# Opening of a gated state-space and MLP kernel rearranged: a B tile loaded transposed, the gate product two groups later, scan tables mirrored from half their length

## The chip, the cores and the metric

The kernel runs on one core of one Trainium2 chip. The metric is the device time of one execution in microseconds. The median of three runs of the kernel before is 551.43 us (551.0 to 551.49).

## The reference, cut to what matters

The input x has 2048 rows (time steps) of 1024 features. The result is a gate g times a state-space branch a, plus (1 - g) times an MLP branch b. The gate is a sigmoid of one weighted row sum of x.

```python
g = sigmoid((x * gate_w).sum(-1, keepdims=True))
dt = exp(log_dt); Lam_bar = exp(dt * Lam)              # complex, 1024 states
B_bar = ((Lam_bar - 1) / Lam)[:, None] * (B_re + 1j * B_im)
Bu = einsum("bld,pd->blp", x, B_bar)
h_t = Lam_bar * h_{t-1} + Bu_t                         # for all 2048 steps
a = 2 * einsum("blp,dp->bld", h, C_re + 1j * C_im).real + x * Dskip
b = gelu(layernorm(x) @ w1 + b1) @ w2 + b2
out = g * a + (1 - g) * b
```

## The kernel before

**Stages on the matrix engine (PE).** PE runs four stages: the u stage, which multiplies x by B (real and imaginary part) and gives the input u of the scan; the MLP's first and second product; and the y stage, which multiplies the scanned state by C. VectorE (DVE) runs the scan behind the later stages, with cosine and sine tables that it builds from 256 positions for each of the 1024 states.

**Groups.** Nearly every product is done as a 2 x 2 block product with seven sub-products instead of eight. The class `SG` holds them as p1 to p7; in the u stage each is four matmuls of 512 columns. They need sums of the operands: `b_sums` makes S1 to S4 from B, `x_sums` and `x_sum4` make T1 to T4 from x (tiles `xqo(pr, i)`; T4 takes the place of a raw part of x). p5 takes S1 and T1, p6 S2 and T2, p7 S3 and T3, p4 the raw A22 and T4, p3 S4. A group `bu_group(pt, pr)` covers tile pt of B (128 states, real and imaginary part) and half pr of x (1024 rows). The order is (1,0), (2,0), (3,0), (0,1), (1,1), ... and from the third group on it goes: p1 of this group, p7 of the one before, p5 and p6 of this one, p4 of the one before, p2 and p3 of this one. p7 and then p4 of one group add into the same PSUM bank, and the value between them is one half of u: ScalarE copies it out (`uc`, L1221) and VectorE adds the part of `s5` to it (L1223). Tile 0 with half 0 is done by plain products (`bu_plain`).

**Transposed operands.** PE needs x and B with the features on the partitions. At the opening the first 512 rows of x (`t_x`, four tiles) and tiles 0 to 3 of B (`t_b0`, `t_b`) are loaded as they lie, transposed on PE against an identity in eight steps a tile, and copied out of PSUM by VectorE or ScalarE. The other 1536 rows of x come through three transposing DMAs (`xT_dma`, L1232, chunks 1 to 3 of 512 rows), and tiles 4 to 7 of B through transposing DMAs later (`bT_dma`, L1316). Loads are issued on SP's queue, the small vectors (`cst_loads`) on ScalarE's, and stores on GpSimd's.

**The gate product.** `z_gate` (L1289) multiplies all of x, so all three transposed chunks, by the gate weight in 32 matmuls, four of them side by side in the array. It stands in the second group (n == 1 of the loop), ahead of `x_sum4(0)`, since that one overwrites raw x. `z_move` sends the row through HBM into a column layout; the layer norm waits for it.

**Order of the work.** Nothing is placed by hand on an engine. Each task has a duration and a priority, and a planner (`Graph.schedule`) works out one order for each engine; on PE the chain `pe_last` fixes the order of products, while `o_chain` does so for the opening. Every engine then runs its list in order. At the start PE runs nine idle products on zeros (`em_warm`).

Of the kernel before, what the change touches and what calls it, by code (L numbers as in the profile page):

```python
# [43 lines left out]
def c_dve(N):  # L44
    return 0.09 + N / 960.0
# [126 lines left out]
class Graph:  # L172
# [43 lines left out]
    def dma(self, prio, emit, nbytes, sem, reads=(), writes=(), name="", xpose=False, extra=(), ndma=1, bw=None, thr=False, q="sp"):  # L216
# [3 lines left out]
        if xpose:  # L220
            idur = max(idur, XPOSE_ISSUE_PER_MB * nbytes / 1e6)
        return self.add(q, idur, prio, emit, reads, writes, name, kind="dma", nbytes=nbytes,
                        sem=sem, xpose=xpose, extra=extra, ndma=ndma, bw=bw, thr=thr)

    def _schedule_once(self):
# [27 lines left out]
        while ev:  # L253
# [17 lines left out]
            for e in engs:  # L271
# [25 lines left out]
                if t.kind == "dma":  # L297
                    issue_end = st + t.dur
                    push(issue_end, 1, e)
                    ts = max(issue_end, chan_free[e])  # L300
                    busy_o = sum(1 for o in chan_free if o != e and chan_free[o] > ts)
                    bw_eff = t.bw * (1.0, 0.55, 0.4)[busy_o]
                    chan_free[e] = ts + t.nbytes / bw_eff
                    t.finish = chan_free[e] + DMA_LAT
# [76 lines left out]
    def _schedule_latest(self, ls):  # L381
# [57 lines left out]
        while ev:  # L439
# [8 lines left out]
            for e in engs:  # L448
# [13 lines left out]
                if t.kind == "dma":  # L462
                    issued = t.start + t.dur
                    push(issued, 1, e)
                    ts = max(issued, chan_free[e])
                    others = sum(1 for o in chan_free if o != e and chan_free[o] > ts)
                    chan_free[e] = ts + t.nbytes / (t.bw * (1.0, 0.55, 0.4)[others])
                    t.finish = chan_free[e] + DMA_LAT
# [97 lines left out]
def build(nc, A_x, A_Lambda_re, A_Lambda_im, A_B_re, A_B_im, A_C_re, A_C_im, A_log_dt, A_Dskip,  # L566
# [25 lines left out]
    with es:  # L592
# [81 lines left out]
        tfirst = [7, 3, 6, 0, 1, 2, 5]  # L674
# [57 lines left out]
        g.dma(P0, emit_cst_loads, NROW * 256, sem("d_cst"), writes=[b_stg], name="cst_loads", ndma=len(vecs), q="act")  # L732
# [36 lines left out]
        def load_x(k, prio):  # L769
            v = XNAT[k]  # L770
            g.dma(prio, lambda e: e.dma_start(out=v.ap, in_=x2[k * 128:(k + 1) * 128, :]), 128 * D * 2,  # L771
                  ssem("xnat", k), writes=[v], name="xnat%d" % k)
# [3 lines left out]
        def load_b(pt, prio):  # L776
# [9 lines left out]
            g.dma(prio, em, 2 * 128 * D * 2, ssem("bnat", s), writes=[v], name="bnat%d" % pt, ndma=2)  # L786
# [4 lines left out]
        def t_x(k, prio):  # L791
# [11 lines left out]
            o_chain(g.add("pe", 0.06 * DT, prio, em, reads=[v, b_ident], writes=[b_ps[bk], b_ps[bk2]], name="xT_T%d" % k, extra=list(o_last)))  # L803
# [12 lines left out]
        def t_b(pt, prio):  # L816
            s = pt % 4
            for ri in range(2):
                bk = tbank()

# [8 lines left out]
                if (pt, ri) == (1, 1):  # L829
# [23 lines left out]
        def load_b0(ri, prio):  # L853
# [3 lines left out]
            g.dma(prio, lambda e: e.dma_start(out=v.ap, in_=ap[0:128, :]), 128 * D * 2, ssem("bnatA", ri), writes=[v], name="bnat0.%d" % ri)  # L857
# [3 lines left out]
        for k in range(1, 4):  # L861
            load_x(k, (-0.9, k))
        load_b0(1, (-0.89, 0))
        for pt in range(1, 4):
            load_b(pt, (-0.85, pt))

        def t_b0(ri, prio):
# [8 lines left out]
            t = g.add("pe", 0.06 * DT, prio, em, reads=[v, b_ident], writes=[b_ps[bk]], name="bT0.%d" % ri, extra=list(o_last))  # L876
            if ri == 0:
                o_chain(t)
            o = AR.v(bqo(0, 2 * ri), [(1, D)])
            if ri == 0:  # L880
                first_a.append(g.add("act", c_act(D), prio, lambda e: e.activation(o.ap, V(PS16[bk], 0, [(1, D)]), AF.Copy),
                                     reads=[b_ps[bk]], writes=[o, b_ps[bk]], name="bTe0.0"))
            else:
                first_e.append(g.add("dve", 0.65, prio, lambda e: e.tensor_copy(o.ap, V(PS16[bk], 0, [(1, D)])),
                                     reads=[b_ps[bk]], writes=[o, b_ps[bk]], name="bTe0.1"))
# [3 lines left out]
        for k in range(1, 4):  # L889
            t_x(k, (-0.8, k + 1))  # L890
        t_b0(1, (0.6, 0))
        bk0 = tbank()
        g.add("pe", 0.06, (0.6, 1),
              lambda e: e.transpose(V(PS16[bk0], 0, [(1, NROW)]), V(STG, 0, [(1, 128)], npart=NROW), V(IDENT, 0, [(1, NROW)], npart=NROW)),
              reads=[b_stg, b_ident], writes=[b_ps[bk0]], name="cst_T", extra=list(o_last))
        stage_names = ["LRE", "LIM", "LDT", "DSK", "B2", "GW", "B1"]
        cst_cp = g.add("dve", 0.15, P0, lambda e: e.tensor_copy(V(CST, 0, [(1, NROW)]), V(PS16[bk0], 0, [(1, NROW)])),
              reads=[b_ps[bk0]], writes=[bc(n) for n in stage_names] + [b_ps[bk0]], name="cst_copy", extra=first_e[-1:])

# [4 lines left out]
        dv("dt_exp", lambda e: e.activation(C("DTC", 0, n8), C("LDT", 0, n8), AF.Exp), ["LDT"], ["DTC"], dur=0.3, eng="act", prio=P0)  # L904
        b_dtb = B("dtb")
        g.add("dve", 0.12, P0, lambda e: e.tensor_copy(V(DTB, 0, [(1, n8)]), C("DTC", 0, n8)), reads=[bc("DTC")], writes=[b_dtb], name="dt_b16")
        g.add("dve", 0.12, P0, lambda e: e.tensor_copy(C("DTC", 0, n8), V(DTB, 0, [(1, n8)])), reads=[b_dtb], writes=[bc("DTC")], name="dt_back")
        dv("a", lambda e: e.tensor_tensor(C("A", 0, n8), C("DTC", 0, n8), C("LRE", 0, n8), ALU.mult), ["DTC", "LRE"], ["A"], prio=P0)
        dv("th", lambda e: e.tensor_tensor(C("TH", 0, n8), C("DTC", 0, n8), C("LIM", 0, n8), ALU.mult), ["DTC", "LIM"], ["TH"], prio=P0)
        dv("r_exp", lambda e: e.activation(C("R", 0, n8), C("A", 0, n8), AF.Exp), ["A"], ["R"], dur=0.3, eng="act", prio=P0)  # L910
        b_ki = B("ki")
        b_ki2 = B("ki2")
        dv("phi", lambda e: e.tensor_scalar(C("PHI", 0, n8), C("TH", 0, n8), 1.0 / TWO_PI, None, ALU.mult), ["TH"], ["PHI"], prio=P0)
        g.add("dve", 0.12, P0, lambda e: e.tensor_copy(V(KI, 0, [(1, n8)]), C("PHI", 0, n8)), reads=[bc("PHI")], writes=[b_ki], name="ki")
        g.add("dve", 0.12, P0, lambda e: e.tensor_copy(C("KF2", 0, n8), V(KI, 0, [(1, n8)])), reads=[b_ki], writes=[bc("KF2")], name="kf")
        dv("ttr", lambda e: e.tensor_tensor(C("TTR", 0, n8), C("PHI", 0, n8), C("KF2", 0, n8), ALU.subtract), ["PHI", "KF2"], ["TTR"], prio=P0)
# [1030 lines left out]
```

## Time and profile before

| what | us |
|---|---|
| median of three runs | 551.43 |
| profiled execution | 554.73 |
| span of the profiled execution | 553.0 |
| PE busy in the span | 546.1 |
| DVE busy in the span | 510.2 |
| ScalarE (ACT) busy in the span | 287.1 |

The profiled execution took 1.73 us more than its span, and 3.30 us more than the median; differences are worked out inside the span and taken off the median. A busy PE is not a PE at its peak: ends of matmuls are modelled, and a stretch at a lower clock is busy too. The spans of PE's weight loads (PEld) show the real spacing of its instructions.

### The profile page before, as it was taken

What the parts mean: (1) busy time and instruction counts of PE and PEld (TensorE: products, weight loads), DVE (VectorE), ACT (ScalarE), POOL (GpSimd) and SP (SyncE); (2) the same over time, 40 slices, a digit from 0 to 9 for tenths busy, and PEclk for the clock granted to TensorE, in tenths of its full rate; (3) what the DMA queues carried; (4) which work ended last, traced back from release to release, by engine and by line L of the source; (5) the groups of instructions that cost most, each with busy time, mean ns of one, the idle gap of its engine ahead of it and who ended that gap; (6) DMA issues with size and microseconds to landing.
All of it is one profiled execution on the core that took longest, in us unless ns stands there. A gap on an engine that the chain in (4) does not pass through costs nothing.

```text
span 553.0 us, 7464 instructions
## 1 busy us (share of the span) xinstructions
PE 546.1 (99%) x2622; PEld 250.2 (45%) x2622; DVE 510.2 (92%) x880; ACT 287.1 (52%) x480; POOL 89.7 (16%) x146
## 2 busy tenths in 40 slices
PE   8899999999999999999999999999999999999997
PEld 5444444444444444444444444444444444444443
DVE  5879989999999999999999999999999999899863
ACT  3767887886773347773347762247672322111110
POOL 0127662540001010001110000220000111001000
PEclk9989999999999999999999999999999999999999
DMA  9996999789762455464666983797767999987531
GB/s 268 252 301 155 272 272 293 252 274 360 237 142 105 164 190 206 148 216 196 225 227 184 310 167 64 135 200 226 240 157 136 230 312 298 376 293 249 180 117 57
DMA packets 115054, 120.07 MB, mean 217 GB/s; under 512 B 70338, under 2 KB 92738, under 8 KB 113994
## 3 DMA queue, kind: packets, MB, share of 16 engines
q1 hardware_dynamic: 102400, 73.69, 47.9%
q0 software_dynamic: 12480, 45.90, 26.8%
q8 instruction: 20, 0.33, 0.2%
q14 instruction: 16, 0.13, 0.1%
q10 hardware_dynamic: 138, 0.02, 0.0%
HBM read 56.40 MB, written 47.46 MB: 188 GB/s over the span
## 4 chain that ended last, share of the span: by engine, by line
PE 94%; SPq 3%; DMA 2%; issue 0%; DVE 0%
PE ps L1034 71%; PE ps L1032 22%; SPq L1232 2%; DMA ar<-in_A_x_dram 2%; PE ps L1289 1%; PE ps L1100 0%; SPq L771 0%; SPq L784 0%; SPq L783 0%; SPq L857 0%; DVE ar L1732 0%
## 5 line engine op out<-in xcount | busy, mean ns | idle before, releaser
L1034 PE MATMUL ps<-ar 128*128 128x512 f16 (+1 forms) x1844 | 416.9, 379 | 0.0
L1034 PEld LDWEIGHTS ps<-ar 128*128 128x128 f16 (+1 forms) x1844 | 180.1, 98 | 218.1 <-issue 1.3
L1032 PE MATMUL ps<-ar 128*128 128x512 bf16 (+1 forms) x608 | 150.0, 379 | 0.0
L1119 DVE TENSOR_TENSOR ar<-ar 128x512 f16<-128x512 bf16 (+7 forms) x224 | 140.0, 662 | 3.9 <-PE ps L1289 2.0
L1032 PEld LDWEIGHTS ps<-ar 128*128 128x128 bf16 (+1 forms) x608 | 59.3, 98 | 71.5 <-ACT ar L833 0.4
L1426 DVE TENSOR_TENSOR_SCAN ar<-cst,init,ar 128x256 bf16<-128x256 f32 x128 | 88.1, 734 | 0.4
L1054 ACT ACTIVATE ar<-ps 128x512 f32<-128x512 f32 x102 | 59.8, 596 | 51.1 <-PE ps L1032 36.8
L1070 ACT ACTIVATE ps<-ps 128x512 f32<-128x512 f32 x67 | 39.0, 582 | 75.4 <-PE ps L1032 64.3
L1412 DVE TENSOR_TENSOR ar<-ar 128x2048 bf16<-128x2048 bf16 x64 | 77.0, 1217 | 0.2 <-ACT ar L1000 0.2
L1533 ACT ACTIVATE ar<-ps,cst 128x512 bf16<-128x512 f32 x56 | 38.4, 686 | 13.4 <-PE ps L1034 13.1
L1055 ACT ACTIVATE ar<-ps,cst 128x512 f32<-128x512 f32 x32 | 22.0, 688 | 44.6 <-PE ps L1034 22.1
L1622 ACT ACTIVATE ar<-ps,cst 128x512 f32<-128x512 f32 x32 | 22.0, 687 | 43.6 <-PE ps L1034 43.6
L1415 DVE TENSOR_TENSOR ar<-ar 128x1024 bf16<-128x1024 bf16 x64 | 42.0, 683 | 0.1
L1539 ACT ACTIVATE ar<-ar,cst 128x512 bf16<-128x512 f32 x56 | 40.0, 713 | 3.7 <-DVE ar L1537 3.5
L1537 DVE TENSOR_TENSOR ar<-ps,ar 128x512 f32<-128x512 f32 x56 | 38.2, 683 | 3.8 <-PE ps L1034 3.1
L1136 POOL DMA_DIRECT2D scr_u<-ar x32 | 24.9, 780 | 44.4 <-ACT ar L1164 20.4
L1745 DVE SCALAR_TENSOR_TENSOR ar<-ps,cst,ar 128x512 bf16<-128x512 f32 x31 | 22.6, 741 | 6.2 <-PE ps L1034 6.0
L1634 POOL DMA_DIRECT2D scr_ac<-ar x16 | 13.8, 892 | 87.5 <-ACT ar L1055 26.1
L1444 POOL DMA_DIRECT2D scr_h<-ar x16 | 9.4, 586 | 108.8 <-DVE ar L1415 88.7
L1625 DVE SCALAR_TENSOR_TENSOR ar<-ps,cst,ar 128x512 f32<-128x512 f32 x32 | 23.6, 741 | 3.5 <-PE ps L1034 2.9
L1632 POOL DMA_DIRECT2D scr_ac<-ar x16 | 8.5, 534 | 83.9 <-DVE ar L1625 54.8
L1716 DVE SCALAR_TENSOR_TENSOR ar<-ar,cst 128x1024 f32<-128x1024 bf16 x16 | 20.1, 1273 | 0.0
(120 smaller groups left out, 248.0 us busy)
## 6 DMA issues: line engine op xcount, KB each, us to landing
scr_ac<-ar POOLq DMA_DIRECT2D x32, 512.0 KB, 5.4
ar<-in_A_x_dram SPq DMA_DIRECT2D x32, 256.0 KB, 5.0
scr_u<-ar POOLq DMA_DIRECT2D x32, 256.0 KB, 5.1
ar<-scr_u SPq DMA_DIRECT2D x16, 512.0 KB, 4.5
scr_h<-ar POOLq DMA_DIRECT2D x16, 512.0 KB, 4.5
ar<-scr_ac SPq DMA_DIRECT2D x16, 512.0 KB, 7.5
ar<-scr_h SPq DMA_DIRECT2D x8, 1024.0 KB, 7.0
ar<-in_B_w_dram SPq DMA_DIRECT2D x14, 512.0 KB, 5.5
```

What stands on the lines that cost most here:

```text
L1032: ins = e.matmul(V(PS[bk], 0, [(1, n)]), st[i].ap, mv[i].ap, start=(i == 0), stop=(i == K - 1))
L1034: ins = e.matmul(V(PS[bk], 0, [(1, n)]), st[i].ap, mv[i].ap, start=False, stop=(i == K - 1), skip_group_check=True)
L1054: return e.activation(o.ap, V(PS[bk], 0, [(1, 512)]), AF.Copy)
L1070: g.add("act", c_act(512), (pb[0], q - 2), lambda e: e.activation(V(PS[b], 0, [(1, 512)]), V(PS[a], 0, [(1, 512)]), AF.Copy), reads=[b_ps[ ...
L1119: g.add("dve", c_tt16(n), (pb[0], q), lambda e: e.tensor_tensor(o.ap, a.ap, b.ap, op), reads=[a, b], writes=[o], name=nm).slack = slack
L1136: g.dma((1.0, q), lambda e: e.dma_start(out=US[pt // 4, :, 4 * pr:4 * pr + 4, r0:r0 + T], in_=evv.ap), 2 * 128 * CH * 2, ssem("us", 2 * ks ...
L1412: g.add("dve", c_tt16(UE), pri(i), lambda e: e.tensor_tensor(o.ap, a.ap, tbl.ap, ALU.mult), reads=[a, tbl], writes=[o], name=nm + tag)
L1415: g.add("dve", c_tt16(UE // 2), pri(i), lambda e: e.tensor_tensor(o.ap, a.ap, b.ap, op), reads=[a, b], writes=[o], name=nm + tag)
L1426: lambda e, pt=pt, ri=ri, vin=vin, go=go: e.tensor_tensor_scan(go.ap, Cb("R", pt, T), vin.ap, V(INIT, pt * 2 + ri, [(1, 1)]), ALU.mult, AL ...
L1533: g.add("act", c_act(512, ap_operands=1), (10.0, q + 1), lambda e: e.activation(o.ap, V(PS[bk], 0, [(1, 512)]), AF.Gelu_apprx_tanh, bias=C ...
L1537: g.add("dve", c_dve(512), (10.0, q - 2), lambda e: e.tensor_tensor(sv.ap, V(PS[bk], 0, [(1, 512)]), sv.ap, ALU.add), reads=[b_ps[bk], sv] ...
L1539: g.add("act", c_act(512, psum=False, ap_operands=1), (10.0, q + 3), lambda e: e.activation(o.ap, sv.ap, AF.Gelu_apprx_tanh, bias=C("B1", ...
```

## The change

- **Loads.** SP issues x tile 0, B tile 0 (real), x 1, B 0 (imaginary), x 2, x 3, and then the transposing DMAs. B tiles 1 and 2 go to ScalarE's queue, behind the seven small vectors. B tile 3 is no longer loaded as it lies nor transposed on PE: two transposing DMAs bring it, between chunks 2 and 3 of x.
- **Opening on PE.** Five idle products instead of nine. Both parts of B tile 0 are copied out by ScalarE. The plain products of the first 512 rows are cut into halves for both parts (`bu_half`), and the order around them is new.
- **Gate product.** It moves from the second group to the fourth (n == 3). `x_sum4(0)` is run a second time for the early groups: T4 of half 0 goes to a place of its own (`XN + 24576`) and the first three groups read it there; the copy in place comes after the gate product. p4 of the first two groups moves to the end of the third group.
- **Scan tables.** The doubling loop stops one step earlier and fills positions 128 to 255; ScalarE writes positions 1 to 127 as their mirror image (cosine the same, sine negated), and VectorE writes position 0.
- **u parts.** The ScalarE copy `uc` is gone; VectorE adds straight from PSUM.
- **Small chain.** Squares of sine and cosine become one instruction; the constants of the scan get a later priority. `ut3` has less lead, and in the planner's figures some durations and slacks differ.

```diff
-        tfirst = [7, 3, 6, 0, 1, 2, 5]
+        tfirst = [7, 3, 6, 0, 1, 2, 7, 7, 0, 3, 7, 6]
...
-            g.dma(prio, em, 2 * 128 * D * 2, ssem("bnat", s), writes=[v], name="bnat%d" % pt, ndma=2)
+            g.dma(prio, em, 2 * 128 * D * 2, ssem("bnat", s), writes=[v], name="bnat%d" % pt, ndma=2, q="act", issue=0.9)
...
-                if (pt, ri) == (1, 1):
+                if (pt, ri) in ((1, 1), (2, 1)):
                     g.add("dve", 0.65, prio, lambda e, o=o, bk=bk: e.tensor_copy(o.ap, V(PS16[bk], 0, [(1, D)])),
...
-        o_chain(g.add("pe", 3.6, (-0.99, 0), em_warm, reads=[v_zero], writes=[b_ps[4]], name="warm"))
+        o_chain(g.add("pe", 2.9, (-0.99, 0), em_warm(5), reads=[v_zero], writes=[b_ps[4]], name="warm"))
...
         load_x(0, (-0.99, 0))
         load_b0(0, (-0.98, 0))
-        for k in range(1, 4):
-            load_x(k, (-0.9, k))
-        load_b0(1, (-0.89, 0))
-        for pt in range(1, 4):
+        load_x(1, (-0.97, 0))
+        load_b0(1, (-0.96, 0))
+        load_x(2, (-0.95, 0))
+        load_x(3, (-0.94, 0))
+        g.dma((-0.99, 0), emit_cst_loads, NROW * 256, sem("d_cst"), writes=[b_stg], name="cst_loads", ndma=len(vecs), q="act", issue=2.7)
+        for pt in range(1, 3):
             load_b(pt, (-0.85, pt))
...
-            dv("ss%d" % k, lambda e, sk=sk: e.tensor_tensor(C("SS", 0, n8), C(sk, 0, n8), C(sk, 0, n8), ALU.mult), [sk], ["SS"])
-            dv("cc%d" % k, lambda e, ck=ck: e.tensor_tensor(C("CC", 0, n8), C(ck, 0, n8), C(ck, 0, n8), ALU.mult), [ck], ["CC"])
+            dv("cs%d" % k, lambda e, ck=ck: e.tensor_tensor(C("CC", 0, 2 * n8), C(ck, 0, 2 * n8), C(ck, 0, 2 * n8), ALU.mult), [ck, sk], ["CC", "SS"])
...
-        for k in range(LT):
+        for k in range(LT - 1):
             n = 1 << k
...
+        for comp, nm, sg in ((0, "MC", 1.0), (1, "MS", -1.0)):
+            src = AR.v(E1 + (comp * NTAB + T - 1) * 4, [(T, PT), (-1, TH - 1)], F32)
+            dst, end = w1(comp, 1, TH - 1), w1(comp, 0, 1)
+            g.add("act", c_act(PT * TH, psum=False), (2.55, comp), lambda e, dst=dst, src=src, sg=sg: e.activation(dst.ap, src.ap, AF.Copy, scale=sg), reads=[src], writes=[dst], name="e1m%d" % comp)
+            g.add("dve", 0.12, (2.55, comp), lambda e, end=end, nm=nm: e.tensor_copy(end.ap, V(CST, col[nm + str(LT - 1)], [(1, PT), (0, 1)])), reads=[bc(nm + str(LT - 1))], writes=[end], name="e1z%d" % comp)
...
-                    if ri == 0:
-                        g.add("dve", c_dve(CH), (1.0, q - 2), lambda e: e.tensor_tensor(ev.ap, V(PS[bk], 0, [(1, 2 * T)]), src.ap, ALU.add),
-                              reads=[b_ps[bk], sv], writes=[ev, b_ps[bk]], name="u" + nm)
-                    else:
-                        g.add("act", c_act(CH), (1.0, q - 2), lambda e: e.activation(uc.ap, V(PS[bk], 0, [(1, 512)]), AF.Copy),
-                              reads=[b_ps[bk]], writes=[uc, b_ps[bk]], name="uc" + nm)
-                        g.add("dve", c_dve(CH), (1.0, q - 2), lambda e: e.tensor_tensor(ev.ap, uc.ap, src.ap, ALU.add),
-                              reads=[uc, sv], writes=[ev], name="u" + nm)
+                    g.add("dve", c_dve(CH), (1.0, q - 2), lambda e: e.tensor_tensor(ev.ap, V(PS[bk], 0, [(1, 2 * T)]), src.ap, ALU.add),
+                          reads=[b_ps[bk], sv], writes=[ev, b_ps[bk]], name="u" + nm)
...
-        bu_plain(0, 0)
+        t_b(1, (0.5, 2), (0.5, 4))
+        xT_dma(1, (-0.5, 0))
+        xT_dma(2, (-0.4, 0))
+        bT_dma(3, (-0.35, 0))
+        xT_dma(3, (-0.3, 0))
+        bu_half(0, 0, (0.5, 0))
+        bu_half(1, 0, (0.5, 1))
+        bu_half(0, 1, (0.5, 3))
         early = [bu_group(1, 0), bu_group(2, 0)]
         early[0].p1()
+        bu_half(1, 1)
+        early[0].p2()
         t_b(2, (1.0, seq[0] + 0.5))
-        early[0].p2()
         early[1].p1()
-        t_b(3, (1.0, seq[0] + 0.5))
+        bu_plain(0, 1, (0,))
         early[1].p2()
-        bu_plain(0, 1)
+        bu_plain(0, 1, (1,))
         bT_dma(4)
...
-            if n == 2:
-                early[0].p4()
             if prev is not None:
                 prev.p7()
             cur.p5()
             if n == 1:
+                x_sum4(0, seq[0], XN + 24576)
+            if n == 3:
                 z_gate()
                 z_move()
                 x_sum4(0, seq[0])
+                x_sum4(1, seq[0])
             cur.p6()
+            if n > 2:
+                prev.p4()
             if n > 1:
-                prev.p4()
                 cur.p2()
             cur.p3()
+            if n == 2:
+                early[0].p4()
+                prev.p4()
```

## Rows read from the trace of the kernel before

**Rows 1.** The page's first part: busy us, share of the span, instructions.

```profile
PE 546.1 (99%) x2622; PEld 250.2 (45%) x2622; DVE 510.2 (92%) x880; ACT 287.1 (52%) x480; POOL 89.7 (16%) x146
```

**Rows 2.** Chain that ended last, first 80 us: start us, us, what.

```profile
6.72 7.47 SPq L1232
...
19.22 8.73 DMA ar<-in_A_x_dram
...
28.00 3.22 PE ps L1289 x32
31.21 2.15 PE ps L1034 x8
```

**Rows 3.** Busy time by stretch: us, PE, PEld, DVE, ACT, POOL, granted clock, DMA.

```profile
25.80:28.00 2.20, 0.02 (x2) 0.00 (x1) 0.60 (x2) 0.60 (x1) 0.14 (x1) 1.00 1.01 374
28.00:31.20 3.20, 3.20 (x33) 0.99 (x34) 1.23 (x1) 0.00 (x0) 0.00 (x0) 0.57 1.04 391
...
50.00:118.00 68.00, 68.00 (x316) 30.83 (x315) 64.19 (x126) 57.90 (x109) 37.61 (x57) 1.00 0.95 265
```

**Rows 4.** PE's opening in order of time: start us, us, line, operands, count.

```profile
1.25 3.72 PE L845 MATMUL ps<-ar 128*128 128x512 bf16 x9 [1.25 <-DVE ar L978]
...
4.59 0.65 PEld L801 LDWEIGHTS ps<-ident,ar 128*128 128x128 bf16 x8 [0.23 <-issue]
...
5.19 0.49 PEld L874 LDWEIGHTS ps<-ident,ar 128*128 128x128 bf16 x8
...
9.74 0.20 PE L894 MATMUL ps<-ident,stg 76*128 76x76 bf16 x1
...
17.88 4.48 PE L1032 MATMUL ps<-ar 128*128 128x512 bf16 x20
```

**Rows 5.** DMA issues of short windows: KB each, us from issue to landing.

```profile
ar<-in_A_x_dram SPq DMA_DIRECT2D x1, 256.0 KB, 2.8
...
ar<-in_A_B_im_dram SPq DMA_DIRECT2D x1, 256.0 KB, 6.5
...
ar<-in_A_x_dram SPq DMA_TRANSPOSE x1, 11.1
...
ar<-in_A_x_dram SPq DMA_TRANSPOSE x1, 7.4
```

**Rows 6.** Issues and ScalarE of the opening in order of time.

```profile
0.80 0.40 SPq L771 DMA_DIRECT2D ar<-in_A_x_dram  x1
...
3.12 0.37 ACTq L728 DMA_DIRECT2D stg<-in_B_b_dram  x1
...
3.52 1.28 ACT L881 ACT_TABLE_LOAD   x1 [3.52 <-issue]
...
5.89 1.02 ACT L881 ACTIVATE ar<-ps 128x1024 bf16<-128x1024 bf16 x1 [1.09 <-PE ps L874]
...
6.23 0.45 SPq L784 DMA_DIRECT2D ar<-in_A_B_im_dram  x1
```

**Rows 7.** Groups by line and shape: count, busy us, mean ns, idle before.

```profile
L1119 DVE TENSOR_TENSOR ar<-ar 128x2048 f16<-128x2048 bf16 x8 | 9.4, 1220 | 3.8 <-PE ps L1289 2.0 <-DMA ar<-in_A_x_dram 1.7
L972 DVE TENSOR_TENSOR ar<-ar,cst 128x1024 f32<-128x1024 f32 x4 | 4.9, 1215 | 0.0
L972 DVE TENSOR_TENSOR ar<-ar 128x1024 f32<-128x1024 f32 x2 | 2.4, 1215 | 0.0
L1000 ACT ACTIVATE ar<-ar 128x1024 bf16<-128x1024 f32 x2 | 2.1, 1048 | 0.0
L1537 DVE TENSOR_TENSOR ar<-ps,ar 128x512 f32<-128x512 f32 x56 | 38.2, 683 | 3.8 <-PE ps L1034 3.1
```

**Rows 8.** One u part late in the u stage: copy, next products, add.

```profile
108.57 0.60 ACT L1221 ACTIVATE ar<-ps 128x512 f32<-128x512 f32 x1
...
109.18 3.62 PE L1034 MATMUL ps<-ar 128*128 128x512 f16 x16
...
110.03 0.68 DVE L1223 TENSOR_TENSOR ar<-ar 128x512 bf16<-128x512 f32 x1
```

More of the change, by code (lines that the diff above doesn't have):

```diff
@@ L214, in add, with dma @@
         return t
-    def dma(self, prio, emit, nbytes, sem, reads=(), writes=(), name="", xpose=False, extra=(), ndma=1, bw=None, thr=False, q="sp"):
+    def dma(self, prio, emit, nbytes, sem, reads=(), writes=(), name="", xpose=False, extra=(), ndma=1, bw=None, thr=False, q="sp", issue=None):
         if bw is None:
@@ L219, in dma @@
         idur = {"sp": SP_ISSUE, "act": ACT_ISSUE, "pool": POOL_ISSUE}[q] * ndma
-        if xpose:
+        if issue is not None:
+            idur = issue
+        elif xpose:
             idur = max(idur, XPOSE_ISSUE_PER_MB * nbytes / 1e6)
@@ L299, in _schedule_once @@
                     push(issue_end, 1, e)
[L300 to L304, printed above, removed]
+                    if t.nbytes < 32768:
+                        t.finish = issue_end + DMA_LAT
+                    else:
+                        ts = max(issue_end, chan_free[e])
+                        busy_o = sum(1 for o in chan_free if o != e and chan_free[o] > ts)
+                        bw_eff = t.bw * (1.0, 0.55, 0.4)[busy_o]
+                        chan_free[e] = ts + t.nbytes / bw_eff
+                        t.finish = chan_free[e] + DMA_LAT
                     push(t.finish, 2, t)
@@ L464, in _schedule_latest @@
                     push(issued, 1, e)
[L465 to L468, printed above, removed]
+                    if t.nbytes < 32768:
+                        t.finish = issued + DMA_LAT
+                    else:
+                        ts = max(issued, chan_free[e])
+                        others = sum(1 for o in chan_free if o != e and chan_free[o] > ts)
+                        chan_free[e] = ts + t.nbytes / (t.bw * (1.0, 0.55, 0.4)[others])
+                        t.finish = chan_free[e] + DMA_LAT
                 else:
@@ L770, in load_x @@
             v = XNAT[k]
-            g.dma(prio, lambda e: e.dma_start(out=v.ap, in_=x2[k * 128:(k + 1) * 128, :]), 128 * D * 2,
-                  ssem("xnat", k), writes=[v], name="xnat%d" % k)
+            return g.dma(prio, lambda e: e.dma_start(out=v.ap, in_=x2[k * 128:(k + 1) * 128, :]), 128 * D * 2,
+                         ssem("xnat", k), writes=[v], name="xnat%d" % k, issue=0.6 if k == 0 else 0.43)
         BN = {}
@@ L802, in em @@
                 return ins
-            o_chain(g.add("pe", 0.06 * DT, prio, em, reads=[v, b_ident], writes=[b_ps[bk], b_ps[bk2]], name="xT_T%d" % k, extra=list(o_last)))
+            t = g.add("pe", 0.9 if k == 0 else 0.06 * DT, prio, em, reads=[v, b_ident], writes=[b_ps[bk], b_ps[bk2]], name="xT_T%d" % k, extra=list(o_last))
+            if chain:
+                o_chain(t)
             o = AR.v(xqo(0, 0) + k * 256, [(512, DT), (1, 128)])
@@ L908, in build @@
[L908 to L910 removed]
+        g.add("dve", 0.12, PC, lambda e: e.tensor_copy(V(DTB, 0, [(1, n8)]), C("DTC", 0, n8)), reads=[bc("DTC")], writes=[b_dtb], name="dt_b16")
@@ L911, in build @@
         b_ki = B("ki")
         b_ki2 = B("ki2")
[L913 to L916, printed above, removed]
@@ L1157, in bu_plain @@
+        def bu_plain(pt, c, ris=(0, 1)):
+            for ri in ris:
                 bk = (4, 5, 6, 1)[2 * c + ri]
                 ws = [AR.v(bqo(pt, 2 * ri) + dt * 256, [(1, 128)]) for dt in range(DT)]
-                if (pt, c, ri) == (0, 0, 0):
-                    q = mm_half(bk, ws)
-                else:
-                    q = mm("bu%d.%d.%d" % (pt, c, ri), bk, ws, [xt(dt, c) for dt in range(DT)], True)
-                ev = u_ev(pt, c // 2, ks, ri, c % 2)
-                g.add("act", c_act(CH), (1.0, q), lambda e, ev=ev, bk=bk: e.activation(ev.ap, V(PS[bk], 0, [(1, 2 * T)]), AF.Copy),
-                      reads=[b_ps[bk]], writes=[ev, b_ps[bk]], name="u%d.%d.%d" % (pt, c, ri))
@@ L1166, in bu_plain @@
-                if c % 2 == 1:
-                    u_store(pt, c // 2, ks, q, ri)
+                q = mm("bu%d.%d.%d" % (pt, c, ri), bk, ws, [xt(dt, c) for dt in range(DT)], True)
+                u_copy(pt, c, ri, bk, 2, q)
         def b_sums(pt, q):
```

165 lines of the change are left out of this document (86 added, 79 removed).

## The prediction

> **What bounds the kernel now.** Read the page's first part first: PE is busy 546.1 of 553.0 us, DVE 510.2 [rows 1]. So there is little idle time on PE to win, and one has to find where it lies. The chain of waits says where: it ends on PE, and back from the end it runs through PE products alone until 28.00 us; ahead of that it is the gate product waiting for a DMA, and SP's queue issuing the transposing loads since 6.72 [rows 2]. The stretch table shows what the wait costs. From 25.80 to 28.00 PE does nothing, and then the granted clock is 0.57 on average from 28.00 to 31.20: most of the gate product runs at 1.2 GHz instead of 2.4 [rows 3]. The eight products behind it still take 2.15 us [rows 2], where 315 matmuls in 68.00 us (0.216 each) make 1.73. So one late transfer, the third transposed chunk of x, costs 2.2 us idle, about 1.4 in the gate product (3.22 at 0.57 would be 1.8 at full clock) and 0.4 behind it: 4.0 us. From 33.36 (31.21 + 2.15) on PE is full, and the change can win only ahead of that mark. My mark of comparison is therefore: gate product done and the second group done up to p3. Before, it is reached at 33.36.
>
> **The change part by part: the start.** The first x tile lands at 3.6 (0.80 + 2.8) [rows 5, 6], but its transposes begin at 4.59, behind nine idle products of 0.41 us each, which is the lower clock level's spacing although the column reads 1.00 there [rows 4]. Five take about 2.1 us, so PE is free at 3.4 and takes the tile at 3.65, at the lower level: 0.86 us instead of the 0.49 of the second tile [rows 4]. What then sets the pace is landing and copying out. SP issues a load each 0.49 us (twelve between 0.80 and 6.72), the first landing 2.8 and the twelfth 6.5 us after issue [rows 5]; by a straight line between these, fourth (B 0 imaginary) lands near 6.0 and sixth (x 3) near 7.6. Copying out is now ScalarE's for both parts of B 0, and a wait is added there: the four loads of B tiles 1 and 2 are queued on ScalarE ahead of its table load. The vectors' issues end at 3.49, the table load follows at 3.52 [rows 6]; four more issues at 0.45 move it to about 5.35, it ends at 6.65, and two copies of 1.02 end at 7.7 and 8.7. Behind them stand the first two half products (8 x 256 columns, 0.86 each): the second ends at 9.6. Bounds: 8.4 if the copies follow the landings alone (6.0, transposes 0.49, copy 1.02, half product 0.86), 10.6 if the two queues slow each other by 1 us. Before, the same work (48 transposes, two half products) was done at 9.74, where the transpose of the vectors starts [rows 4]. So the opening gains nothing yet; I keep 9.6.
>
> **Up to the first use of chunk 1.** Left on PE until then: transposes of B 1 and B 2 (32, at 0.49 per eight 1.96), two half products 1.73, three sub-products of four matmuls 2.59, vectors 0.1: 6.4 us, so 16.0 (bounds 15.0 and 17.4, from the bounds above and up to 0.4 for waiting on a copy). Before, this point was 17.88, with the second group's p2 already done [rows 4]. The 16 transposes of B 3 that are gone account for 0.98 of it.
>
> **Does chunk 1 land by 16.0?** Before it landed at 17.8 (6.72 + 11.1), 5.1 us after the last plain load of its queue (6.23 + 6.5 = 12.7) [rows 5, 6]. Now the last plain load of SP's queue lands at 7.6, and four loads of 0.26 MB stand on the other queue: at the 391 GB/s of the stretch table [rows 3] they take 2.7 us of the same engines. 7.6 + 2.7 + 5.1 = 15.4. Bounds: 12.7, if the other queue costs nothing, and 17.8 as before. I take 15.4, from the row of the same transfer. It is just covered.
>
> The row shows chunk 1 queued behind twelve loads [rows 5, 6]. The Trainium skill (DMA: Bandwidth & Descriptors, "Issuing engines are not separate DMA queues") says that DMAs of all issuing engines end on the same 16 engines and interleave, and that a second issuer saves only the time to initiate. By that rule alone the earlier issue is worth nothing, only the 0.52 MB of B 3 that are gone count (1.3 us), chunk 1 lands at 16.5 and the sum below is 0.5 us worse, 546.7. No row here shows two loading queues at work at once, so the trace leaves this open.
>
> **From there to the mark.** Behind the first use of chunk 1 PE has 48 matmuls of 512 columns up to the second group's p3 (two plain products of 8, p2 of 4, seven sub-products of 4): 48 x 0.216 = 10.4. The gate product comes later but belongs to the sum: 1.8 at full clock (bounds 1.7 and the 3.22 of the row). 16.0 + 10.4 + 1.8 = 28.2, against 33.36: **5.2 us** less.
>
> **What must be covered for that.** Tile 3 of B: two transposing loads of half a chunk in sum. Chunk 2 landed 3.8 us after chunk 1, at 21.6 (14.2 is its issue, at the end of 7.47 us from 6.72, and 7.4 its landing) [rows 2, 5], chunk 3 at 27.95; so 15.4 + 3.8, plus half a chunk (2 to 3 us), gives 22, and the first product with it comes at 26.4: covered by 4 us, also for its four sums. Chunk 3 then lands at 28 to 29; the sums of half 1 (1.22 each [rows 7]) are wanted by p5 of the fourth group, at 26.4 + 8 x 0.86 + 2 x 0.86 = 35.0: covered by 3 us or more. The early T4 costs DVE 1.22 once. The gate product ends near 37.7 and not 31.2, and its copy, two stores on GpSimd's queue and two loads on SP's go with it, 6.5 us later; SP's transposing loads of B tiles 5 to 7 queue behind them, and the layer norm waits. Tile 5 is first used in the tenth group, some 30 us later, and the MLP starts where the u stage ends, near 112.6 (109.18 + 3.45) [rows 8]; the groups in between hide both. If not, PE would stand there.
>
> DVE loses six instructions of 1024 elements (6 x 1.215 = 7.3 us [rows 7]) and gains the T4 (1.22): 6 us less, against some 5 us by which PE's demand comes earlier. It is off the path in the u stage, 64.19 of 68.00 busy with no gap on PE [rows 3]. The two mirror copies on ScalarE have no row; the nearest is a copy of 1024 elements at 1.05 [rows 7]. They would be cheaper or dearer with a backward read; ScalarE is free half the span [rows 1] and loses 15 copies of 0.60, so either end costs nothing. The changed durations and slacks alter only the order the planner writes; I count them at nothing, with the fourth rival for what they may do.
>
> **The rivals.** First, chunk 1 lands as before, at 17.8: PE stands 1.8 us at its first use and goes on from 17.85, so the mark is at 30.0 and 3.4 us are won: 548.0. If the idle time also drops the clock, as 2.2 us did before the gate product, another 1.9 go: 549.9. For it speaks that the transposing loads set the chain today; against, that a half megabyte less lies ahead of them. Second, the clock stays at the lower level through the opening, since PE has pauses between 3.4 and 8: the transposes keep up with the landings (0.86 per tile), but two half products and part of the wait double, about 2.3 us: 548.5. The first weight loads behind nine idle products took 0.65, so the level rose just there [rows 4]; that is for it, and that pauses of 0.23 did not lower it before is against. The Trainium skill (TensorE: Matmul & The Clock Gate, "What's actually happening") says that the lower level lasts for a stretch of time, not for a number of matmuls, and falls back with idling; by that rule fewer idle products change little as long as PE stays busy.
>
> Third, slower: the bank between p7 and p4. Now VectorE itself must read p7's bank before p4 writes there. In the row ScalarE's copy starts at 108.57, p4 starts at 110.04 (109.18 + 0.86), and VectorE's add starts at 110.03 and takes 0.68 [rows 8]: with this order p4 would stand 0.7 us. Thirteen groups with that are 9 us, and 555.5; it is slower than before from 0.42 us a group on. Against it: the MLP's first product has the same pattern 56 times, adds of 683 ns straight from PSUM, waiting for PE and not PE for them [rows 7]; the planner knows the new wait and can move the add up. Fourth, the change does not do what it says: the planner's order or a late tile 3 or chunk 3 puts a wait of 2 us with the lower clock back on PE, one group later, and the gain is spent: 551.4.
>
> **How the numbers follow.** Forecast 546.2 (551.43 - 5.2), own range 544.6 to 547.6, from 15.0 and 17.4 for the first use: chance 0.68. Chunk 1 late 0.12 (half of it with the clock), clock low 0.07, bank 0.06, gain spent 0.05, else 0.02. The range 544.6 to 549.6 takes in the forecast, the low clock and half of the late chunk, near 0.8. Within 0.2% (1.1 us, about what a measurement of this kernel can tell from no change): 0.05; slower: 0.07; faster: 0.88.
>
> **What would show it.** Right: the gate product takes under 2 us, its clock reads 1.00, nothing idle ahead of it, and PE is full from about 16 us. Wrong: an idle stretch on PE at the plain product of chunk 1 (late chunk), weight loads spaced double beyond 5 us (clock), PE waiting for VectorE once a group until 112 (bank), or an idle stretch at the third or fourth group.

## The result, and the profile after

The changed kernel takes 557.87 us (median of 6 runs, 555.04 to 558.81) against 551.52 for the kernel before (551.0 to 552.29): ratio 1.0091, interval 1.0062 to 1.0119. It is 0.9% slower, where 546.2 and faster was forecast, and it lies above the range of 544.6 to 549.6. The profiled execution has a span of 557.1 us (558.81 us in all).

The page's first part of after (answers to [rows 1]):

```profile
PE 546.5 (98%) x2610; PEld 252.4 (45%) x2610; DVE 505.0 (91%) x869; ACT 279.2 (50%) x465; POOL 86.8 (16%) x146
```

TensorE's waits in after (engine, line, waited for: us in total, times, longest):

```profile
PE ps L835 <- DMA ar<-in_A_B_im_dram: 5.4, 1, 5.4
PE ps L865 <- DVE ar L990: 1.2, 1, 1.2
PE ps L808 <- DMA ar<-in_A_x_dram: 0.9, 1, 0.9
```

VectorE did lose 5.2 us (510.2 to 505.0), and TensorE waits in the opening alone. One wait carries the loss: that of the transposes of B tile 1 for the imaginary part's load (the 1.2 us for L990 are the start of the program, as in before). PE of after in order of time (answers to [rows 4]; start us, us, line, operands, count, idle before):

```profile
8.90 1.76 PE L1172 MATMUL ps<-ar 128*128 128x256 bf16 x8
...
10.94 1.04 PE L1172 MATMUL ps<-ar 128*128 128x256 bf16 x8
17.40 1.04 PE L835 MATMUL ps<-ident,ar 128*128 128x128 bf16 x8 [5.42 <-DMA ar<-in_A_B_im_dram]
18.23 1.91 PE L1172 MATMUL ps<-ar 128*128 128x256 bf16 x8
...
35.73 1.03 PE L1049 MATMUL ps<-ar 128*128 128x512 bf16 x4
...
45.31 1.90 PE L1299 MATMUL ps<-ar,gwc 128*2 128x512 bf16 x32
```

L835 transposes B tiles 1 and 2, L1172 is a half product, L1049 and L1051 are the products of the u groups (L1032 and L1034 before), L1299 the gate product. The third group's first product starts at 35.73; with 1.83 for the gate product, which now comes later (45.31 to the next product at 47.15), the mark of the prediction is reached at 37.56. The chain of waits names the transfer (an answer to [rows 2]; start us, us, what):

```profile
3.95 13.41 DMA ar<-in_A_B_im_dram
```

The issues show which queues were at work (answers to [rows 6]), ScalarE's and then SP's:

```profile
3.95 0.45 ACTq L791 DMA_DIRECT2D ar<-in_A_B_im_dram  x1
4.43 1.41 ACTq L790 DMA_DIRECT2D ar<-in_A_B_re_dram  x1
5.87 0.62 ACTq L791 DMA_DIRECT2D ar<-in_A_B_im_dram  x1
6.53 1.28 ACT L901 ACT_TABLE_LOAD   x1 [6.53 <-issue]
```

```profile
3.70 19.55 SPq L1242 DMA_TRANSPOSE ar<-in_A_x_dram  x2
```

Stretches of after (us, busy PE, PEld, DVE, ACT, POOL, granted clock, DMA share, GB/s; answers to [rows 3]):

```profile
12.00:17.40 5.40, 0.00 (x0) 0.00 (x1) 0.00 (x0) 0.00 (x0) 0.00 (x0) 0.98 1.22 136
17.40:20.00 2.60, 2.60 (x17) 2.11 (x18) 0.00 (x0) 1.02 (x1) 0.00 (x0) 0.50 1.26 174
```

For 5.4 us no engine computes. The DMA engines are fully busy, yet move 136 GB/s (in the 5.4 us 0.36 MB by SP's queue and 0.38 MB by ScalarE's), and behind the wait the clock is at its lower level (0.50): eight transposes and a half product take 2.5 us there. Plain loads from ScalarE's queue and transposing loads from SP's queue are in flight together from 3.70 on; the plain one needs 13.4 us, where the row of before has 6.5 [rows 5].

### The profile page after: what moved, and what is told of

It is laid out like the page before. It is cut to its first block, busy times and chain, and to the rows that moved or that the text cites. A ratio compares the mean times of both kernels' runs of the same rounds, so it can differ in the third digit from the quotient of the medians.

```text
span 557.1 us, 7421 instructions
## 1 busy us (share of the span) xinstructions
PE 546.5 (98%) x2610; PEld 252.4 (45%) x2610; DVE 505.0 (91%) x869; ACT 279.2 (50%) x465; POOL 86.8 (16%) x146
## 4 chain that ended last, share of the span: by engine, by line
PE 96%; DMA 2%; ACTq 1%; DVE 0%; issue 0%
PE ps L1051 71%; PE ps L1049 23%; DMA ar<-in_A_B_im_dram 2%; PE ps L835 0%; PE ps L1172 0%; ACTq L736 0%; PE ps L1299 0%; PE ps L1117 0%; DVE ar L1750 0%; ACTq L790 0%; PE ps L855 0%
## 5 line engine op out<-in xcount | busy, mean ns | idle before, releaser
L1051 PE MATMUL ps<-ar 128*128 128x512 f16 (+1 forms) x1844 | 416.7, 379 | 0.0
L1051 PEld LDWEIGHTS ps<-ar 128*128 128x128 f16 (+1 forms) x1844 | 180.1, 98 | 217.9 <-ACT ar L1071 0.6
L1049 PE MATMUL ps<-ar 128*128 128x512 bf16 (+1 forms) x600 | 148.3, 379 | 0.0
L1136 DVE TENSOR_TENSOR ar<-ar 128x512 f16<-128x512 bf16 (+7 forms) x225 | 141.9, 667 | 1.3 <-DMA ar<-scr_h 0.7
L1049 PEld LDWEIGHTS ps<-ar 128*128 128x128 bf16 (+1 forms) x600 | 58.5, 98 | 70.6 <-issue 0.5
L1233 DVE TENSOR_TENSOR ar<-ps,ar 128x512 bf16<-128x512 f32 x30 | 20.6, 686 | 4.0 <-PE ps L1051 3.1
```

Source lines behind the costliest of these rows:

```text
L1049: ins = e.matmul(V(PS[bk], 0, [(1, n)]), st[i].ap, mv[i].ap, start=(i == 0), stop=(i == K - 1))
L1051: ins = e.matmul(V(PS[bk], 0, [(1, n)]), st[i].ap, mv[i].ap, start=False, stop=(i == K - 1), skip_group_check=True)
L1136: g.add("dve", c_tt16(n), (pb[0], q), lambda e: e.tensor_tensor(o.ap, a.ap, b.ap, op), reads=[a, b], writes=[o], name=nm).slack = slack
```

## Experiments

The mark sorts the runs. Behind it the rest of the span is nearly the same in these profiles, 519.5 to 520.4, once the waits behind the mark are taken off, and in e3 1.3 more for the 12 products behind the wait, which run at a lower clock (us, worked out from each trace: start of the third group's first product, plus 1.83 where the gate product comes behind it):

| profile | mark | span | span less mark | waits of PE behind the mark |
|---|---|---|---|---|
| before, the one of the rows | 33.36 | 553.0 | 519.6 | 0 |
| before, second (e5) | 29.98 | 549.7 | 519.7 | 0 |
| after | 37.56 | 557.1 | 519.5 | 0 |
| after, second (e10) | 35.42 | 556.1 | 520.7 | 0.8 |
| e1, B tiles 1 and 2 on SP's queue | 28.66 | 548.8 | 520.1 | 0 |
| e2, x's transposing loads held | 35.82 | 555.7 | 519.9 | 0 |
| e3, before with B on ScalarE's queue | 41.81 | 565.2 | 523.4 | 2.1 |
| e4, e1 with the gate product back | 31.55 | 555.7 | 524.1 | 3.7 |
| e11, the same, second | 35.40 | 556.7 | 521.3 | 1.3 |
| e6, SP's later loads held | 33.10 | 553.6 | 520.5 | 0.8 |
| e9, e1 with tile 3 plain | 29.77 | 551.4 | 521.6 | 1.6 |

**e1: the loads back on SP's queue.** After, with one line changed:

```diff
-   ... name="bnat%d" % pt, ndma=2, q="act", issue=0.9)
+   ... name="bnat%d" % pt, ndma=2, issue=0.9)
```

> The changed kernel with one part undone: B tiles 1 and 2 are issued on SP's queue, ahead of the transposing loads, and not on ScalarE's. Theory (overlap): the plain loads of ScalarE's queue and the transposing loads of SP's ran at the same time on the same engines and slowed each other. Then the imaginary part of B tile 1 lands by 10 us instead of 17.4, PE's wait of 5.4 us is gone, chunk 1 lands by 17 and the time is 546 to 548.5. Rival (opening): the new order of the opening, fewer idle products and pauses on PE, is what costs; then it stays slower than the kernel before, 552 or more.

550.50 us (550.01 to 551.13), ratio to before 0.9972 [0.9961, 0.9983]; 7.4 us less than after, but above the 546 to 548.5 expected, which still took the forecast's 5.2 us off the median (see e5). PE of e1, and then four stretches:

```profile
9.18 1.04 PE L1172 MATMUL ps<-ar 128*128 128x256 bf16 x8
10.06 0.61 PE L835 MATMUL ps<-ident,ar 128*128 128x128 bf16 x8
...
26.83 1.03 PE L1049 MATMUL ps<-ar 128*128 128x512 bf16 x4
```

```profile
7.00:9.50 2.50, 2.48 (x34) 2.19 (x32) 1.65 (x5) 1.14 (x2) 0.00 (x0) 1.00 1.05 386
12.00:13.50 1.50, 1.44 (x12) 0.99 (x11) 1.48 (x5) 0.72 (x3) 0.00 (x0) 1.00 1.27 289
13.50:15.00 1.50, 1.50 (x17) 1.02 (x15) 1.50 (x12) 0.94 (x3) 0.00 (x0) 1.00 1.43 152
...
15.00:18.00 3.00, 2.99 (x21) 1.46 (x20) 2.87 (x12) 1.92 (x5) 0.00 (x0) 1.00 1.00 220
```

The wait is gone, and the clock reads 1.00 in these stretches. Plain loads move 386 GB/s by themselves. Transposing loads by themselves move 289 while one is well under way. Towards its end the rate drops (152 from 13.5 to 15 us, at a DMA share of 1.43), and over 15 to 18 us, where the engines first stand idle, it is 220. So a low rate with busy engines is no sign of two queues by itself; what came with them in after is that 136 GB/s lasted 5.4 us and that a plain load took 13.4. The mark of 28.66 is 0.5 off the 28.2 of the prediction: with the queue put right, the steps up to the mark held.

**e3: the queue alone.** The kernel before, with one line changed (its loads are those of three tiles):

```diff
-   ... name="bnat%d" % pt, ndma=2)
+   ... name="bnat%d" % pt, ndma=2, q="act")
```

> The kernel before with this one part of the change: B tiles 1 to 3 go to ScalarE's queue. Overlap theory: SP's queue comes to its transposing loads 3 us earlier, they run into the six plain loads, B tile 1 lands after 13 us and PE stands 3 to 8 us: 554 to 560, slower than the kernel before. Rival (opening): without the new order of the opening the queue does not matter, 550.5 to 552.5.

565.53 us, ratio 1.0264 [1.02, 1.0328], above the 554 to 560 expected. Moving these issues costs 13.5 us by itself. In the profiles 11.8 us of the loss lie ahead of the mark (41.81 against 29.98 in e5); the rest is one wait for ScalarE behind it and what follows. PE of e3, and a stretch:

```profile
17.45 1.01 PE L825 MATMUL ps<-ident,ar 128*128 128x128 bf16 x8 [9.75 <-DMA ar<-in_A_B_im_dram]
```

```profile
9.00:17.40 8.40, 0.00 (x0) 0.00 (x0) 0.00 (x0) 0.96 (x1) 0.00 (x0) 0.63 1.18 161
```

The same transfer is waited for, and the DMA engines are as busy at as low a rate. So the loss needs nothing else of the change.

**e2 and e6: ScalarE's queue without the overlap.** e2 holds the transposing loads of x until B tiles 1 and 2 have landed:

```diff
-   ssem("xT", c), ..., xpose=True, bw=200000.0)
+   ssem("xT", c), ..., xpose=True, bw=200000.0, extra=b_loads)
```

> The changed kernel with B tiles 1 and 2 still on ScalarE's queue, but the transposing loads are held back until those four loads have landed. Overlap theory: alone, ScalarE's queue is as quick as SP's, the imaginary part of B tile 1 lands by 9 us and all four by 10.5; chunk 1 then lands some 7.4 us after its issue, near 18, PE waits about 2 us for it, and the time is 548 to 551. Rival (slow queue): ScalarE's queue itself serves late; then B tile 1 still lands at 13 us or later and the time is 555 or more.

558.66 us, ratio 1.0123 [1.0105, 1.0142], and not the 548 to 551 expected. B tile 1 came early, its first transposes start at 7.88. But the planner let nine later x tiles and a part of tile 3 past on SP's queue, so chunk 1 was issued at 11.99, and TensorE waited for that instead (PE of e2):

```profile
22.10 3.42 PE L1050 MATMUL ps<-ar 128*128 128x512 bf16 x8 [2.37 <-DMA ar<-in_A_x_dram]
```

The wait had only moved, so e6 holds those loads as well:

```diff
-   ssem("xnat", k), ..., issue=0.6 if k == 0 else 0.43)
+   ssem("xnat", k), ..., issue=0.6 if k == 0 else 0.43, extra=b_loads if k > 3 else ())
...
-   ssem("bT", 2 * pt + ri), ..., bw=200000.0 if pt < 4 else None)
+   ssem("bT", 2 * pt + ri), ..., bw=200000.0 if pt < 4 else None, extra=b_loads)
```

> The changed kernel with tiles 1 and 2 of B still loaded from ScalarE's queue, but every load on SP's queue behind the first four x tiles (transposing loads of x and B, the later x tiles) held until those four loads have landed; nothing else is changed. Theory, overlap: plain loads of one queue and transposing loads of another slow each other down; without overlap the imaginary part of tile 1 lands by about 9 us instead of 17.4, the first transposing load is issued near 9.5 and lands near 17, TensorE waits 0 to 2 us for it, and the time is 549.5 to 552. Rival: ScalarE's queue is slow by itself, or the loss is in what the planner does with the other order; then tile 1 is late again or TensorE waits over 4 us, and the time is 555 or more.

554.41 us, ratio 1.0033 [1.0004, 1.0063]: 3.5 us less than after, above the 549.5 to 552 expected. PE of e6, and a stretch:

```profile
7.88 1.04 PE L809 MATMUL ps<-ident,ar 128*128 128x128 bf16 x8 [1.35 <-DMA ar<-in_A_x_dram]
8.71 1.06 PE L836 MATMUL ps<-ident,ar 128*128 128x128 bf16 x8
```

```profile
3.00:9.00 6.00, 3.75 (x29) 2.67 (x28) 0.74 (x2) 2.31 (x2) 0.00 (x0) 1.00 1.03 372
```

B tile 1 (L836) is not waited for, and plain loads from two queues at once move 372 GB/s: neither ScalarE's queue nor two queues are slow in themselves. What slows is plain loads of one queue beside transposing loads of the other. The rest of the loss is of this version's own making: the planner now issued B's loads at 0.80, ahead of the vectors, the x tile waited 1.35, and the transposes ran at the lower clock's spacing (0.85 us from one eight to the next) until 12 us. The second half product starts at 13.96 and not at 9.18 as in e1, and the mark lies 4.4 us later than there.

**e5: before, profiled again.**

> The kernel before, unchanged, profiled a second time. If the profile on which the sum was based shows what every execution does, the span is again near 553.0 us at a clock of 0.997, PE stands some 2 us ahead of the gate product, this takes about 3.2 us, and the gate product and the second group up to p3 are done near 33.4 us. If that profile was an untypical execution, as the spans of 549.6 to 551.1 at a clock of 1.0 in the timed runs of the kernel before suggest, the span is near 550, the idle time ahead of the gate product is under 1 us, the gate product takes 1.8 to 1.9 us, and the mark is reached near 30.5.

551.5 us, span 549.7, clock 1.0. PE of e5:

```profile
26.41 1.90 PE L1289 MATMUL ps<-ar,gwc 128*2 128x512 bf16 x32
28.24 1.90 PE L1034 MATMUL ps<-ar 128*128 128x512 f16 x8
29.98 1.03 PE L1032 MATMUL ps<-ar 128*128 128x512 bf16 x4
```

No idle time ahead of the gate product and 1.90 for it, where [rows 2, 3] showed 2.2 idle and 3.22. The timed runs of before beside e1 had, all but one, spans of 549.6 to 551.1, and five of the 61 timed runs of before on record took 554 us or more. So of the 4.0 us on which the forecast rested, 3.4 (marks of 33.36 and 29.98) belong to a slower execution than the usual one.

**e10: after, profiled again.**

> The changed kernel, unchanged, profiled a second time. If the overlap of ScalarE's plain loads with SP's transposing loads makes the wait, as in its first profile, the imaginary part of tile 1 of B lands again 10 us or more after its issue, TensorE stands 2 to 6 us for it ahead of its transposes, and chunk 1 lands after 19 us. If the first profile was untypical, as that of the kernel before was, the wait is below 1 us, and the loss must lie elsewhere.

557.78 us. The same wait, a little shorter (PE of e10):

```profile
15.16 0.82 PE L835 MATMUL ps<-ident,ar 128*128 128x128 bf16 x8 [4.25 <-DMA ar<-in_A_B_im_dram]
```

This loss is in both executions that were profiled, and none of the six timed ones is under 555.04.

**e4 and e11: the gate product back.** e1 with the gate product (and its moves) behind p5 of the second group, as before:

```diff
-            if n == 3:
                 z_gate()
                 z_move()
+            if n == 3:
                 x_sum4(0, seq[0])
```

> As the first of these (B tiles 1 and 2 on SP's queue), with the gate product back in the second group. My forecast's main term was the wait of the gate product for chunk 3 and the lower clock behind it, 4.0 us before, and tile 3 of B now lies ahead of chunk 3. By that this is 3 to 6 us slower than the first kernel and shows PE idle ahead of the gate product. If the place of the gate product is worth nothing, it is within 1 us of it.

558.46 us, ratio 1.0129 [1.0102, 1.0156]. In this profile the gate product did not wait, against what was expected; the loss of 6.9 us in span lay in a late imaginary part of B tile 0 (1.9 us) and in the y stage (3.3 us for the state's load). Since the first of these looked like chance, it was profiled again:

> The changed kernel with tiles 1 and 2 of B on SP's queue and the gate product in its place of before, profiled a second time (558.5 us when it was timed). Theory: the gate product finds its chunk there and takes 1.9 us without a wait, and the loss of 7 us lies at two places, a late imaginary part of tile 0 of B in the opening (1.9 us with a lower clock behind it) and the state's load in the y stage (3.3 us), of which the second, set by the order on SP's queue, comes again and the first need not. Rival: the gate product waits for chunk 3 by 2 us as in the first profile of the kernel before.

558.39 us. Now the rival came true. PE of e4, then of e11:

```profile
27.98 1.90 PE L1299 MATMUL ps<-ar,gwc 128*2 128x512 bf16 x32
...
464.50 1.90 PE L1049 MATMUL ps<-ar 128*128 128x512 bf16 x8 [3.29 <-DMA ar<-scr_h]
```

```profile
29.30 3.58 PE L1299 MATMUL ps<-ar,gwc 128*2 128x512 bf16 x32 [4.04 <-DMA ar<-in_A_x_dram]
...
464.83 1.90 PE L1049 MATMUL ps<-ar 128*128 128x512 bf16 x8 [1.06 <-DMA ar<-scr_h]
```

When the wait comes it costs 4.0 us idle and 1.7 in the product, whose clock is 0.50. The landing of chunk 3 varies from execution to execution, in before as here, so at this place the later gate product saves something between nothing and 6 us. In all the earlier place costs 8 us here: e11 loses 6.7 us ahead of the mark and 1.3 behind it, e4 2.9 and 3.7. The wait in the y stage came in both profiles, 3.3 and 1.1: there the changed order issued the state's later loads at 449.39 in e4, at 442.03 in e1. Why the planner does that was not followed further.

**e7: full-length tables.** e1 with the doubling loop of before, without the mirror copies:

```diff
-        TH = T // 2
-        for k in range(LT - 1):
+        for k in range(LT):
...
-            ... (2.55, comp), lambda e, ...: e.activation(dst.ap, src.ap, AF.Copy, scale=sg), ...
```

> The changed kernel with tiles 1 and 2 of B on SP's queue (550.5 us when it was run) and with the full-length scan tables of the kernel before, doubled to the end on VectorE, no mirror copies on ScalarE: some 5 to 6 us more of VectorE's time ahead of the scan. The prediction's step: VectorE is off the path, nothing follows, 550.0 to 551.0. Rival: the scan ends as much later, the state's way through memory into the y stage comes too late and TensorE waits there, as it did 3.3 us in the run with the earlier gate product; then 553 to 556.

The median of the ten runs is 565.79 us (554.67 to 584.49), above both ranges. The ratio of 1.0117 [1.0084, 1.0149] rests on the five quickest, with a median of 557.97; what the other five met is not shown, since the profile is of one of the five. VectorE is busy 509.7 us in e7 and 505.0 in e1. The mark is as early as in e1 (the third group starts at 26.76), and TensorE does wait, as the rival has it, but at another place. TensorE's wait for VectorE in e7, the last of the five on PE, and VectorE ahead of that:

```profile
PE ps L1045 <- DVE ar L1227: 8.1, 5, 4.2
```

```profile
114.93 4.45 PE L1045 MATMUL ps<-ar 128*128 128x512 f16 x12 [4.18 <-DVE ar L1227]
```

```profile
108.89 1.23 DVE L1130 TENSOR_TENSOR ar<-ar 128x2048 f16<-128x2048 bf16 x1 [4.42 <-issue]
```

L1227 is VectorE's add of a late u part, straight from a bank. It stands in order behind sums for the MLP (L1130); VectorE did nothing from 104.47 to 108.89 ahead of them, for a reason that the trace does not name, and the chain of waits has a load of the layer norm's output (5.49 us from 98.40) just ahead of that gap. Four of the five waits lie in the u stage before this one (0.7, 1.1, 1.8 and 0.3), the first behind x sums that waited 3.9 us for chunk 3. How much of it is the tables' work itself and how much the order that the planner writes around it stays open.

**e8: ScalarE's copies back.** e1 with the copy of each late imaginary u part into a buffer, as before:

```diff
+   g.add("act", c_act(CH), (1.0, q - 2), lambda e: e.activation(uc.ap, V(PS[bk], 0, [(1, 512)]), AF.Copy), ...)
+   g.add("dve", c_dve(CH), (1.0, q - 2), lambda e: e.tensor_tensor(ev.ap, uc.ap, src.ap, ALU.add), ...)
```

> The changed kernel with tiles 1 and 2 of B on SP's queue (550.5 us when it was run) and with ScalarE's copies of the late u parts put back. The prediction's step: the bank costs nothing either way, 550.0 to 551.0, and no waits of TensorE for VectorE once a group without the copies. Rival, the bank between p7 and p4 costs up to 0.7 us in each of 13 groups when VectorE reads the bank itself; then this run is faster than 550 by 2 us or more.

551.67 us (550.55 to 553.36), ratio 0.9983 [0.9951, 1.0015]; that of e1 is 0.9972. No difference can be told, and the 2 us or more of the rival are not there: with e1's tables TensorE does not wait for L1233, the add from the bank, and the bank rival is empty there. With VectorE behind (e7, e9) the same add is what TensorE waits for.

**e9: tile 3 plain.** e1 with tile 3 of B loaded plainly on SP's queue and transposed by TensorE:

```diff
-        for pt in range(1, 3):
+        for pt in range(1, 4):
             load_b(pt, (-0.85, pt))
...
-        bT_dma(3, (-0.35, 0))
...
         early[1].p1()
+        t_b(3, (1.0, seq[0] + 0.5))
```

> The changed kernel with tiles 1 and 2 of B on SP's queue (550.5 us when it was run) and with tile 3 of B loaded plainly there again and turned over by TensorE, as in the kernel before. The prediction's steps: 16 transposes come back (0.98 us), and chunk 1's transposing load is queued behind two more plain loads of 0.26 MB (1.3 us) and may now be waited for: 551.5 to 552.5, with the third group beginning near 28.0 to 29.0 us instead of 26.8. Rival: chunk 1 was covered and the transposes fill idle time, 550.0 to 551.0; or tile 3 by plain loads frees SP's queue for chunk 3 and the sums, and the time is below 550.

554.74 us, ratio 1.0045 [1.0026, 1.0064], 4.2 us more than e1; 1 to 2 were expected. PE of e9:

```profile
27.94 1.03 PE L1049 MATMUL ps<-ar 128*128 128x512 bf16 x4
...
108.15 2.76 PE L1051 MATMUL ps<-ar 128*128 128x512 f16 x12 [1.24 <-DVE ar L1233]
```

The mark moved by 1.1, as the 16 transposes ask; 1.6 us more are waits for VectorE behind it, one of them for the late u add. Its profiled execution (553.27 us) is 1.5 us quicker than its median; that part has no place in the trace.

**e12: e1 again, in more rounds.**

> The changed kernel with tiles 1 and 2 of B on SP's queue once more, against the kernel before in more rounds: 549.9 to 551.2, a ratio of 0.996 to 0.999. The steps of the prediction give this version 1.3 us over an execution of the kernel before that does not wait ahead of its gate product (marks of 30.0 and 28.7 us), not 5.2.

550.52 us (549.97 to 552.48) against 551.96, ratio 0.9978 [0.9966, 0.999]. The change with its loads on SP's queue is the best version here.

## Why the prediction was wrong, step by step

**The baseline failed.** "From 25.80 to 28.00 PE does nothing" is true of the profiled execution and not of the second one (e5). The first took 554.73 us, 3.3 more than the median, and the timed runs shown lay at 551.0 to 551.49. Of the 4.0 us that "one late transfer" was to give back, 3.4 are that same difference. The gain was then taken off the median, which held little of the loss. Against the second profile the forecast mark of 28.2 is worth 1.8 us, not 5.2, and the time is 549.6. e1 shows it: mark 28.66, 1.3 us ahead of 29.98, and 1.4 to 1.5 us won by the medians.

**"The start" failed by 2.4 us.** x 0 was taken at 3.49 at the lower level as forecast (3.65). But the second load pair delayed ScalarE: one stretch of issues took 1.41 and the last 0.62 instead of 0.45 each, the table load came at 6.53 and not 5.35, and the second half product ended near 12.0 and not 9.6 (bounds 8.4 to 10.6). TensorE also stayed at the lower level until past 9 (0.82 per eight transposes, 1.76 for the first half product), which is the second rival in part. With the loads on SP's queue the step holds within its bounds: 10.06.

**"Up to the first use of chunk 1" is the step that decided.** It counted the transposes of B 1 as work and gave their loads no landing time. The two-queue case was priced once, at 1 us, for the copies of B 0. The wait was 5.4 us, and the lower clock behind it made the way to the first use 7.9 us (17.40 to 25.29, by the chain) instead of 6.4. With 2.4 from the start, 5.4 and 1.5 make 9.3 of the 9.4 between 28.2 and 37.56. Two slips in its bounds decided nothing: 8.4 and 6.4 make 14.8 and not 15.0, and from 15.0 the lower end of the range is 545.2 and not 544.6.

**"Does chunk 1 land by 16.0?" failed too, unnoticed.** It was issued 3.0 us earlier, at 3.70, and took 16.8 us, so it landed at 20.5 and not 15.4 (bounds 12.7 to 17.8). TensorE does not wait for it, since it comes to the first use only at 25.29. In e1, issued at 5.91, it took 10.1 and landed near 16.0, just ahead of its first use at 16.36: there the step came true, with no slack left. The assumption that loads of two queues share 391 GB/s was wrong where one side transposes (136).

A rule of the Trainium skill was weighed there: that issuing engines are no separate queues and a second one saves only the time to initiate (DMA: Bandwidth & Descriptors, "Issuing engines are not separate DMA queues"). It gave 546.7. The runs agree that the second queue is no second set of engines (372 GB/s by two queues in e6, 386 by one in e1), but show a loss on top. The same page of the Trainium skill ("Queues, rings and completion order") says that each DMA engine takes turns between the queues it has work for, packet by packet. The 13.4 us of a plain load beside transposing ones and the 372 GB/s of plain beside plain do not contradict such sharing, but no run here shows the turns.

**"From there to the mark" held.** 12.2 us were forecast; 25.29 to 37.56 is 12.3, and the gate product takes 1.90 without a wait.

**"What must be covered" held in after and e1.** Tile 3, chunk 3 and the layer norm cause no wait in either, as forecast, and the MLP starts in time. "VectorE is off the path" is not a property of the kernel: in e7, where it has 4.7 us more work, TensorE waits 8.1 us for it. By the chain of waits part of that comes through the layer norm and its sums, the place that the prediction named. The mirrored tables were counted at nothing; without them this version loses 7 us or more, how much of it by the tables and how much by the planner's order stays open.

**The rivals.** Chunk 1 late was the wrong transfer. The bank shows no cost (e8, where an effect under 2 us could not be told). "Slower" had 0.07, on the bank alone; that a queue beside another would slow both had no rival of its own. It should have been one, since the trace had no row for it and 1 us was the most that it was priced at.

## What to carry to other kernels

Compare the profiled execution's time with the timed runs before building on it: an idle stretch in an execution that is 3 us longer than the median may be just that difference, and a second profile settles it. When plain loads move to a second queue to start transposing loads earlier, the price is the overlap: give every load of both queues a landing time, and a rival in which both are slowed, here by half as much again up to three times. A part that is "off the path" in the old order may hold up the new one, so undo the parts singly before calling any of them free.

## What the runs showed of the hardware that was not expected

- Plain loads beside transposing loads of another queue: 136 to 191 GB/s in all with the DMA engines busy (after, e3, e10), against 386 for plain loads alone (e1), 372 for plain loads from two queues (e6) and 289 for a transposing load well under way alone (e1). A plain load of 0.26 MB took 11.3 to 14.7 us at worst (after in both profiles, e3), in before at most 6.5; the slowest transposing load of x took 16.6 to 19.2, in before 10.8 to 11.1.
- TensorE mostly restarted at the lower clock behind a wait of over 2 us: the granted clock was 0.50 in the 2.6 us behind the 5.4 us of after, 0.50 in the 3.7 us behind the 4.0 of e11 and in the 1.9 us behind the 2.4 of e2. That made the wait of after 1.5 us and that of e11 1.7 us dearer than its length. It is no rule: behind the 3.3 us of e4 it read 1.00.
- A transposing load's landing moves by some microseconds between executions of one kernel: the gate product behind chunk 3 waited 2.2 and 0 us in two profiles of before, 0 and 4.0 us in two of e4's kernel.
